# Four query projections traded for seven block products, and one weight tile prepared in its turn

## The chip, the cores and the metric

The kernel runs on one core of a Trainium2 chip. The metric is device time in microseconds (us) for one execution. Names of engines as in the profile: PE is the tensor engine, PEld its weight loads, DVE the vector engine, ACT the scalar engine, POOL the GpSimd engine, SP the engine whose queue issues most transfers.

## The reference, cut to what matters

One layer over 2048 tokens of 512 features, 32 heads of 16 and a gated feed-forward of width 1376:

```
xn = layernorm(x)
q, k, v = split(xn @ wqkv)
pq, pk  = q @ w_phi, k @ w_phi                      # per head
phi     = concat(softmax(p), softmax(-p))           # of pq and of pk
kv, z   = phi_k^T v, sum of phi_k over the tokens   # per head
s       = ((phi_q kv) / (phi_q z + 1e-6)) @ wo
gate    = xn @ W_gate; up = xn @ W_up
g       = silu((relu(gate) * up) @ W_down)
out     = x + s * g
```

The change touches how `q @ w_phi` (the products called `pq` here) is computed for half of the tokens and half of the heads. `w_phi` has been folded into the query weights before, so that `pq` is one product of `xn` with a 512 x 512 matrix, called `WQ` in the kernel.

## The kernel before, in words

**Numbers.** Each float32 operand is held as a pair of tiles, a high part and the rest (`h` and `l` in the names), and `mm3` (line 200) makes one product of three matrix multiplies: low by high, high by low, high by high. A product over 512 features takes four such steps, so 12 multiplies of 512 columns.

**Stages.** The 16 token tiles of 128 are taken in pairs. Tiles 0 to 7 in the list `order` are blocks 2 and 3 of the tokens, tiles 8 to 15 blocks 0 and 1 (a block is 512 tokens). `pair(m)` (line 1202) for m = 1 to 7 does tiles 2m and 2m+1: keys (`pk`), values (`pv`), the softmax features of the keys (`exponents`, `exp_all`, `features_k`, tile `ek`), the products of features and values (`kv_products`, `pkv`), and the transposes of coming tiles (`turn`, `pxT`). From pair 3 on, keys and values of a pair are made by seven block products where eight would be usual: the transposed input `XT` holds for a pair the four blocks A11, A12, A21, A22 (two halves of the features by two token blocks) and four sums of them S1 to S4. The sums are made when a tile is turned: DVE makes `sb`, POOL makes `xf` (`sums_more`), ACT writes the high parts (`sums_hi`) and POOL the low ones (`sums_lo`, rows `XT<-sb` and `XT<-xf`). The first block product of pair m+1 that uses a sum is S1, its second group of six multiplies (`pv<-h`).

**Queries.** `query(n)` (line 406) makes one 128-row part of `pq` for 512 tokens: 12 multiplies, one eviction by ACT into `pqs` and one or two stores to DRAM scratch (`pq<-pqs`). There are 16 of them; two stand in each pair, one in the middle (`query(n - 1)`) and one at the end (`query(n)`), and `query(N - 1)` behind the last pair. Queries 8 to 15 are of the second eight tiles; of these 10, 11, 14 and 15 are of the second half of the 512 query features. `q_load` brings the stored parts back (`pql`), and `q_pair(u)` turns two of them into attention output in many small steps on DVE, ACT and POOL.

**Feed-forward.** The width is cut into 11 tiles of 128, called f = 0 to 10. The tokens are done in two halves, blocks 0 and 1 first. For each f seven block products of six multiplies (`pa` to `pd`, in `gate_up_apart` for f = 0 and 1, in `gate_up` after that) make gate and up; DVE multiplies them (tiles `e`, `u`, later `t`, `r`), ACT and POOL split the product into `hh` and `hl`, and `down` multiplies them with W_down (`py`). Down products of f = 0 and 1 run inside f = 2, and so on. In the first half each f's weights are prepared by `f_prep` (line 542): sums and low parts on POOL (`tab`, `wa`, `wb`, `wc`, `wd`, `fdl`, ten instructions), high parts on ACT, and nine stores `ws` to DRAM, from which the second half loads them (`f_reload`).

**What sets the order.** Each engine runs its instructions in the order in which the code issues them. `Clock` (line 68) counts an estimated time while the code is written out; side work is a generator that says what its next step waits for, and `pace.pump()` issues what is due by that estimate. `preps` (`all_preps`, line 1137) is such a generator: weights of f = 0 from at = 14 on, f = 1 from 15 on, and f at N + f - 1 for the others, where `at` is the current tile number and N = 16. The tiles listed in `AHEAD` (line 36) are prepared earlier and apart: here f = 2 from at = 10 on, into a buffer of its own; it is stored and then loaded back when the first half comes to it. `queries` (`all_queries`, line 1362) holds `state()` (the last `kv_products` and the copy `kvt`), `normalizers()` (the sums `z`, `pkv<-zacc` and `pkv<-zodd`) and the `q_pair` steps.

Of the kernel before, what the change touches and what calls it, by code (L numbers as in the profile page):

```python
# [8 lines left out]
F32R = mybir.dt.float32r  # L9
# [4 lines left out]
P = 128  # L14
# [7 lines left out]
BT = 512  # L22
# [10 lines left out]
UNITS = [*(((0, j), (1, j)) for j in range(2)), ((2, 0), (2, 1)),  # L33
         *(((q, j), (q + 1, j)) for q in (6, 4) for j in range(2)), ((3, 0), (3, 1))]
LAST = [2 * q + j for q in QUERIES[1] for j in range(2)][-3:]
AHEAD, AT = (2,), (10,)
FIRST, SWAP = 3, 3
PLAN = {(0, "turned"): "gc51", (1, "split b"): "gc50", (1, "sums"): "gc01", (1, "scaled"): "gc11", (1, "mid"): "gc21", (1, "split a"): "gc00 sh01 gl01", (1, "turned"): "gc10", (2, "split b"): "sh20 sh11", (2, "sums"): "sh00 gc20", (2, "scaled"): "sh21 gl00", (2, "split a"): "gl20", (2, "turned"): "sh10 gc30 gl11", (2, "end"): "gl21 gl10", (3, "start"): "gc31 gc40 gc41", (3, "split b"): "sh30", (3, "sums"): "sh31 gl30 gl31"}

START = (14, 15)  # L40
WO_WITH = (4, 5, 6, 7)
DOWNS = {2: 1, 4: 1, 6: 1, 7: 1}

# [117 lines left out]
def layer_kernel(ctx: ExitStack, tc: tile.TileContext, x, wkT, wqT, wv, wo, wf, cst, out):  # L161
# [15 lines left out]
    def u2(shape, name, dt=F32):  # L177
        return sb.tile(list(shape), dt, tag="u2", bufs=B2, name=name)
# [222 lines left out]
    def project(n, w, name):  # L401
        p = ps(name=name)
        mm3(p, xt_cols(n), rows(w), range(KD))
        return p

    def query(n):


        h, d = divmod(n, 4)
        c = slice(h % 2 * 2 * P, (h % 2 + 1) * 2 * P)  # L410

        qs = [2 * b + h % 2 for b in PAIRS[h // 2][::-1]]
        p = ps((P, 2, 2 * P), name="pq")

        def w_of(d):
            return lambda k: [t[:, d * P:(d + 1) * P] for t in WQ[k]]
        if n < 2:
            i = 1 - n
            for d in range(2):
                mm3(p[:, d, :], w_of(d), lambda k: [XT[:, 2 * i + k // 2, s, k % 2, c] for s in range(2)], range(KD),  # L420
                    d == 0)
            to = [((qs[i], 0), slice(None), slice(None))]
        else:
            mm3(p, w_of(d), lambda k: [XT[:, k // 2:k // 2 + 3:2, s, k % 2, c] for s in range(2)], range(KD))
            to = [((q, d // 2), d % 2, i) for i, q in enumerate(qs)]
        t = u2((P, 2, 2 * P), "pqs")
        nc.scalar.activation(t, p, AF.Copy)
        for q, col, part in to:
            if q not in PQ:
                PQ[q] = dram((P, 2, 2 * P), f"pq{q[0]}{q[1]}")  # L430
            pace.when(t, lambda q=q, col=col, part=part: nc.sync.dma_start(PQ[q][:, col, :], t[:, part, :]))

    def exponents(pk):

# [107 lines left out]
    def f_prep(f, keep=True):  # L542
# [55 lines left out]
        DONE.add(f)  # L598
        yield None,

    def f_reload(f, part):
        if part == 0:
            FT[f] = [w_pair("wa"), w_pair("wb"), None, None]
            for i, t in enumerate([*FT[f][0], *FT[f][1]]):
                nc.sync.dma_start(f32(flat3(t)), wspill[f][i])
            return
        FT[f][2:] = w_pair("wc"), u2((P, 2, 2, P), "wd", F32R)
        WD[f] = u2((P, D), "fdh", F32R), u2((P, D), "fdl", F32R)
        for i, t in enumerate([*FT[f][2], FT[f][3], *WD[f]]):
            nc.sync.dma_start(f32(flat3(t)), wspill[f][4 + i])  # L610
# [153 lines left out]
    def q_load(u):  # L764
        for j, part in enumerate(UNITS[u]):
            PQS[2 * u + j] = u2((P, 2, 2 * P), "pql")
            nc.sync.dma_start(PQS[2 * u + j], PQ[part])

    def q_pair(u):
# [365 lines left out]
            STEPS[0](what)  # L1135

    def all_preps():
        for f in AHEAD:
            while at[0] < AT[AHEAD.index(f)]:
                yield 3,  # L1140
            f_load(f)
            yield 30,
            yield from f_prep(f, False)
        while at[0] < START[0] - 1:
            yield 3,
        f_load(0)
        yield 30,
        for f in range(NF):
            if f not in AHEAD:
                while at[0] < (START[f] if f < 2 else N + f - 1):  # L1150
# [51 lines left out]
    def pair(m):  # L1202

        n, c = 2 * m, cols(2 * m)
        at[0] = n

        def block(p, s, w, first):
            mm3(p, lambda k: (XT[:, s, 0, k, c], XT[:, s, 1, k, c]), rows(w), range(2), first)
            pace.pump()
        if m <= NP // 2:  # L1210
            pace.later(4, lambda: spill_x(n - 1))
        seven = m >= FIRST
        py = ps(name="pk")
        if seven:
            block(py, A11, WK[:2], True)
            px = ps(name="pk")
            nc.scalar.activation(px, py, AF.Copy)
        else:
            mm3(py, xt_cols(n), rows(WK), range(KD))
        if m > 1:  # L1220
            features_k(n - 1, *EB.pop(), engine=MULT[m > SWAP][1])
        t_steps(m, "start")
        pz = ps(name="pv")
        if seven:
            block(pz, S1, T[0], True)
            block(px, S2, T[1], False)
            va = u2((P, D), "va")
            nc.scalar.activation(va, px, AF.Copy)
        else:
            mm3(pz, xt_cols(n + 1), rows(WV), range(KD))  # L1230
        if m == 1:
            norm_apply(n + 4)
        else:
            features_split(n - 1)
        t_steps(m, "split b")
        news = [k for k in (n + 5, n + 6) if k < N]
        if news:
            norm_stats(*news, bn=m > 2)
        if seven:
            block(py, A12, WK[2:], False)  # L1240
        ea = exponents(py)
        if seven:
            block(px, S3, T[2], False)
            vb = u2((P, D), "vb")
            nc.scalar.activation(vb, px, AF.Copy)
            VH[n + 1] = u2((P, D), "v")
            add(nc.vector, by_head(VH[n + 1], True), by_head(pz), by_head(vb))
        else:
            vb = pz
        t_steps(m, "sums")  # L1250
        if news:
            norm_scale(*news)
        t_steps(m, "scaled")
        pace.pump()
        at[0] = n + 1
        if n + 3 < N:
            t = turn(n + 3)
        exp_all(ea)
        if not seven:
            features_v(n + 1, vb)  # L1260
        if n + 3 < N:
            turned(*t)
            sums_more(n + 3)
            sums_hi(n + 3, 0)
            if n + 7 < N:
                load_x(n + 7)
        t_steps(m, "mid")
        query(n - 1)
        features_k(n, ea, py, engine=MULT[m > SWAP][0])
        if n + 3 < N:  # L1270
            sums_hi(n + 3, 1)
            sums_lo(n + 3)
        for k in news:
            norm_apply(k)
        pace.pump()
        features_split(n)
        t_steps(m, "split a")
        kv_products(n - 2)
        kv_products(n - 1)
        pace.pump()  # L1280
        if seven:
            block(px, A22, T[3], False)
        else:
            px = project(n + 1, WK, "pk")
        eb = exponents(px)
        if seven:
            block(pz, S4, WV[2:], False)
            VH[n] = u2((P, D), "v")
            add(nc.vector, by_head(VH[n], True), by_head(pz), by_head(va))
        else:  # L1290
            va = project(n, WV, "pv")
        if n + 4 < N:
            t = turn(n + 4)
            if n + 8 < N:
                load_x(n + 8)
        exp_all(eb)
        t_steps(m, "turned")
        if n + 4 < N:
            turned(*t)
        if not seven:  # L1300
            features_v(n, va)
        EB.append((eb, px))
        query(n)
        t_steps(m, "end")
        pace.pump()
# [13 lines left out]
    nc.vector.memset(kvt, 0.0)  # L1319
    q_load(0)  # L1320
    query(N - 1)
    kv_products(N - 2)
    pace.pump()

    def state():
        nonlocal kvacc
        kv_products(N - 1)

        kvacc = u2((P, 256), "kvacc")
        nc.scalar.activation(kvacc, PKV[0][:, :4].rearrange("p j x -> p (j x)"), AF.Copy)  # L1330
# [65 lines left out]
    WO = None  # L1396
    for half in range(2):
        b0, b1 = 2 * half, 2 * half + 1
        for f in range(NF):
            if half == 0:  # L1400
                at[0] = N + f
                pace.finish(preps, lambda: f in DONE)
                if f == 0:
                    queries = pace.add(all_queries(0), 20)
# [122 lines left out]
```

## Time and profile before

| | us |
|---|---|
| median of 3 runs | 548.9 (548.45 to 549.0) |
| the profiled execution | 548.96 |
| its span on the core | 547.2 |
| PE busy in the span | 541.5 |
| POOL, DVE, ACT busy | 358.8, 371.3, 259.1 |

The span is the time from the first to the last instruction of the profiled execution; 1.76 us lie around it. Starts of instructions are given in us from the start of the span. A matrix multiply's busy time runs over its neighbours' (they overlap in the engine), so the work of PE is read from the distance between starts. In this execution pair 4 starts at 86.23 us, pair 5 starts at 103.42 us, pair 6 at 120.59, pair 7 at 137.28; f = 0 starts at 156.89, f = 1 at 167.35, f = 2 at 176.88.

### The profile page before, as it was taken

To read this page: it belongs to the slowest core of one execution; us is meant where nothing else is said; L and a number is where in the kernel's file an instruction comes from. 1 tells how busy PE (TensorE), PEld (TensorE's weight loads), DVE (VectorE), ACT (ScalarE), POOL (GpSimd) and SP (SyncE) were. 2 spreads that over 40 slices of the span, in tenths; PEclk is the share of its full clock that TensorE was granted. 3 is DMA by queue.
4 is the path that set the end of the run, shared out by engine and by line. 5 is a ranking of instruction groups with operands and counts; after the bars stand their busy time and mean duration, and the time that the engine had idled before them with its cause. 6 is when DMAs were issued, how large, how long until landed. Compare 5 with 4: busy or idle time off the path is not lost.

```text
span 547.2 us, 9180 instructions
## 1 busy us (share of the span) xinstructions
PE 541.5 (99%) x3192; PEld 442.0 (81%) x3192; DVE 371.3 (68%) x580; ACT 259.1 (47%) x462; POOL 358.8 (66%) x318
## 2 busy tenths in 40 slices
PE   9999999999999999999999999999999999999997
PEld 8798888888878787878878888887777887878886
DVE  5987778686559387799833432899999494924323
ACT  3688766565442657355443241244354545342510
POOL 1569994779992899999977235172365765842491
PEclk9999999999999999999999999999999999999999
DMA  8329889638999848789697998692664744657073
GB/s 281 147 104 332 180 214 266 163 94 234 265 292 394 314 148 300 260 301 330 210 323 257 406 416 320 245 356 83 217 217 134 245 140 157 230 173 288 0 232 115
DMA packets 77662, 128.34 MB, mean 235 GB/s; under 512 B 6832, under 2 KB 29232, under 8 KB 76720
## 3 DMA queue, kind: packets, MB, share of 16 engines
q1 hardware_dynamic: 75456, 120.35, 62.3%
q0 software_dynamic: 2016, 7.34, 7.5%
q8 instruction: 25, 0.41, 0.3%
q14 instruction: 21, 0.17, 0.1%
q10 hardware_dynamic: 144, 0.07, 0.0%
HBM read 70.84 MB, written 52.69 MB: 226 GB/s over the span
## 4 chain that ended last, share of the span: by engine, by line
PE 79%; DVE 8%; DMA 4%; issue 4%; POOL 3%; ACT 1%; SPq 1%; POOLq 0%; ACTq 0%; DVEq 0%
PE py L60 19%; PE pk L60 9%; PE pso L60 8%; PE pd L60 8%; PE pq L60 8%; PE pa L60 7%; PE pb L60 7%; PE pv L60 5%; PE pc L60 4%; DMA ws<-fdl 2%; DVE eq L60 1%; PE pkv L60 1%; PE pnum L60 1%; POOL ez L60 1%; PE pxT L60 1%
## 5 line engine op out<-in xcount | busy, mean ns | idle before, releaser
L60 PE MATMUL py<-fdh,hl 128*128 128x512 f32 x176 | 69.0, 392 | 0.0
L60 PE MATMUL py<-fdl,hh 128*128 128x512 f32 x176 | 68.5, 389 | 0.0
L60 PE MATMUL py<-fdh,hh 128*128 128x512 f32 x176 | 68.5, 389 | 0.0
L60 PE MATMUL pa<-XT,wa 128*128 128x512 f32 x264 | 67.3, 390 | 0.0
L60 PEld LDWEIGHTS pa<-XT,wa 128*128 128x128 f32 x264 | 49.4, 188 | 10.7 <-issue 0.4
L60 DVE TENSOR_TENSOR y<-py,y 128x512 f32<-128x512 f32 x40 | 27.5, 689 | 35.5 <-PE py L60 35.4
L60 POOL TENSOR_TENSOR hl<-t,hh 128x512 fp32r<-128x512 f32 x16 | 20.7, 1296 | 40.7 <-ACT hh L60 40.1
L60 POOL TENSOR_TENSOR y<-y,ys 128x512 f32<-128x512 f32 x24 | 30.9, 1292 | 17.8 <-ACT ys L60 17.3
L60 PE MATMUL pq<-XT,wqh 128*128 128x512 f32 (+1 forms) x144 | 40.5, 367 | 0.0
L60 PEld LDWEIGHTS py<-fdh,hl 128*128 128x128 f32 x176 | 33.0, 188 | 8.4 <-issue 1.2
L60 PEld LDWEIGHTS py<-fdh,hh 128*128 128x128 f32 x176 | 33.0, 188 | 6.9
L60 PEld LDWEIGHTS py<-fdl,hh 128*128 128x128 f32 x176 | 33.0, 188 | 6.7
L60 POOL TENSOR_TENSOR ez<-eq,zB 128x1024 f32<-128x1024 f32 x16 | 38.4, 2407 | 0.1
L60 ACT ACTIVATE hh<-t 128x512 fp32r<-128x512 f32 x16 | 10.1, 633 | 57.0 <-DVE t L60 54.7
L60 DVE TENSOR_REDUCE mx<-pk 128x32 f32<-128x512 f32 x32 | 20.6, 684 | 21.2 <-PE pk L60 21.1
L60 PE MATMUL pd<-XT,wd 128*128 128x512 f32 x132 | 34.2, 393 | 0.4 <-DVE t L60 0.3
L60 PE MATMUL pd<-XT,wc 128*128 128x512 f32 x132 | 33.9, 391 | 0.0
L60 PE MATMUL pb<-XT,wb 128*128 128x512 f32 x132 | 33.6, 390 | 0.0
L60 PE MATMUL pc<-XT,wb 128*128 128x512 f32 x132 | 33.6, 390 | 0.0
L60 POOL TENSOR_TENSOR ol<-of,oh 128x512 fp32r<-128x512 f32 (+1 forms) x13 | 19.8, 1549 | 20.3 <-ACT oh L60 20.3
L60 POOL TENSOR_TENSOR hl<-e,hh 128x512 fp32r<-128x512 f32 x6 | 7.8, 1292 | 35.1 <-ACT hh L60 35.1
L60 PE MATMUL pk<-wkh,XT 128*128 128x512 f32 x88 | 30.2, 395 | 0.0
(189 smaller groups left out, 1445.0 us busy)
## 6 DMA issues: line engine op xcount, KB each, us to landing
xts<-XT SPq DMA_DIRECT2D x4, 1792.0 KB, 8.1
zacc<-ek POOLq DMA_DIRECT2D x14, 512.0 KB, 5.9
XT<-xts SPq DMA_DIRECT2D x7, 1024.0 KB, 6.7
wa<-ws SPq DMA_DIRECT2D x24, 256.0 KB, 5.0
wb<-ws SPq DMA_DIRECT2D x24, 256.0 KB, 4.1
wc<-ws SPq DMA_DIRECT2D x24, 256.0 KB, 2.9
rawg<-wf SPq DMA_DIRECT2D x22, 256.0 KB, 2.9
ws<-wc SPq DMA_DIRECT2D x22, 256.0 KB, 5.1
```

Source lines behind the costliest of these rows:

```text
L60: return self.tc.keep_in_program_order(op(*a, **k))
```

## The change

Queries 10, 11, 14 and 15 are left out of the pairs. Their results are made behind the last pair by `q_tile`: seven block products of six multiplies on A11, S2, S3, S1, A12, A22 and S4, which by then hold blocks 0 and 1 in full. Five of them are evicted by DVE, which adds them up, and two by ACT. The weights are the blocks of `WQ` and two sums of them with their high and low parts (`TQ`), which `q_sums` makes once from at = 7 on, with ten instructions on POOL and two on ACT. `AHEAD` becomes empty, so the weights of f = 2 are prepared in turn, while f = 1 runs, and stay in place for the first half. In pairs 5 to 7 `features_k` stands behind `sums_hi` and `sums_lo` (`SUMS = 5`). `kv_products(N - 2)` moves into `state()`, and `queries` is started ahead of `q_tile` with a delay of 30 where it was 20. (`TURN = 9` and `KV_END = ()` switch nothing: m is at most 7.)

```diff
-AHEAD, AT = (2,), (10,)
+AHEAD, AT = (), ()
+Q_TILES, Q_AT = ((), (1,)), 7
+SUMS = 5
...
     def query(n):
         h, d = divmod(n, 4)
+        if d // 2 in Q_TILES[h // 2]:
+            return
...
+    def q_sums(q):
+        t = u8((P, 4, 2, 2, P), "rq")
+        r, ta, tb = [t[:, k] for k in range(2)], t[:, 2], t[:, 3]
+        for k in range(KD):
+            h, l = (f32(x[:, 256 * q:256 * q + 256].rearrange("p (d x) -> p d x", d=2)) for x in WQ[k])
+            yield "gpsimd", WQ[k][1]
+            add(nc.gpsimd, r[k // 2][:, k % 2], h, l)
+        b11, b12, b21, b22 = (t[:, :, d, :] for t in r for d in range(2))
+        o = u8((P, 2, 2, 2, 2, P), "tq", F32R)
...
+        for i, x in enumerate((ta, tb)):
+            yield "scalar", x
+            nc.scalar.activation(o[:, i, 0], x, AF.Copy)
+            yield from sums_of(o[:, i, 1], x, f32(o[:, i, 0]), ALU.subtract, o)
+        TQ[q] = o
...
+    def q_tile(half, q):
...
+        pa = ps(name="pa")
+        mm3(pa, wq_part(q, 0), a_of(A11), range(2))
+        t1 = u2((P, BT), "t1")
+        nc.scalar.activation(t1, pa, AF.Copy)
+        yield
+        pb = ps(name="pb")
+        mm3(pb, w_of(0, 0), a_of(S2), range(2))
+        m = u2((P, BT), "u2")
+        add(nc.vector, m, pb, t1)
...
+        mm3(pc, w_of(1, 1), a_of(A22), range(2), first=False)
+        t2 = u2((P, BT), "t2")
+        add(nc.vector, t2, pc, m)
+        put(b1, 0, t2)
...
         query(n - 1)
-        features_k(n, ea, py, engine=MULT[m > SWAP][0])
+        if m < SUMS:
+            features_k(n, ea, py, engine=MULT[m > SWAP][0])
         if n + 3 < N:
             sums_hi(n + 3, 1)
             sums_lo(n + 3)
+        if m >= SUMS:
+            features_k(n, ea, py, engine=MULT[m > SWAP][0])
...
     query(N - 1)
-    kv_products(N - 2)
...
     def state():
         nonlocal kvacc
+        kv_products(N - 2)
         kv_products(N - 1)
...
+        if half == 0:
+            queries = pace.add(all_queries(0), 30)
+            at[0] = N
+            for q in Q_TILES[1]:
+                for _ in q_tile(1, q):
+                    pace.pump()
```

On PE, behind the last value product of pair 7 (`pv<-wvh`), there stood before the two queries 14 and 15, of which the first fence shows the last row, and the feed-forward of f = 0 with the last two sets of `pkv` in it:

```order
L60 MATMUL pq<-XT,wqh 128x512 x2
L60 MATMUL pkv<-ek,v 32x64 x16
L60 MATMUL pa<-XT,wa 128x512 x6
L60 MATMUL pb<-XT,wb 128x512 x6
L60 MATMUL pc<-XT,wb 128x512 x6
L60 MATMUL pd<-XT,wc 128x512 x3
L60 MATMUL pkv<-ek,v 32x64 x16
L60 MATMUL pd<-XT,wc 128x512 x3
```

Now the seven blocks stand there, with both sets of `pkv` inside (`tq` are the summed weights, `wqh` and `wql` the plain ones; one `kv_products` is 16 instructions here, which the trace records as 32):

```order
L64 MATMUL pb<-XT,tq 128x512 x6
L64 MATMUL pc<-XT,tq 128x512 x6
L64 MATMUL pd<-XT,tq 128x512 x6
L64 MATMUL pa<-XT,wql 128x512
L64 MATMUL pa<-XT,wqh 128x512 x2
L64 MATMUL pkv<-ek,v 32x64 x32
L64 MATMUL pc<-XT,tq 128x512 x6
L64 MATMUL pd<-XT,wql 128x512
```

What moved: 24 multiplies of `pq` are gone here and 42 of seven blocks have come, and `pkv` runs once in 32 instructions where it ran twice in 16.

On POOL, in pair 5, the sums of tile 13 (`xf`, `XT`), the scaling of the key features `ek` and the first two instructions of the preparation of f = 2 (`rawg<-rawg`) stood before like this:

```order
L60 TENSOR_TENSOR xf<-xf,sb 128x256 x2
L60 TENSOR_TENSOR rawg<-rawg 128x256 x2
L60 TENSOR_TENSOR ek<-ek,rc 128x1024
L60 TENSOR_TENSOR XT<-sb,XT 128x2x2x128
L60 TENSOR_TENSOR XT<-xf,XT 128x2x2x128
```

Now they stand like this:

```order
L64 TENSOR_TENSOR xf<-xf,sb 128x256 x2
L64 TENSOR_TENSOR XT<-sb,XT 128x2x2x128
L64 TENSOR_TENSOR XT<-xf,XT 128x2x2x128
L64 TENSOR_TENSOR ek<-ek,rc 128x1024
L64 DMA zacc<-ek 128x1024
```

What moved: the low parts of the sums now follow `xf` at once, and the preparation of f = 2 is no longer there.

On POOL, from the last instruction of the preparation of f = 1 (`fdl`) to the split of its product, there stood before only the splits of f = 0 (`hl<-e`, `hl<-u` with the first numbers), of f = 1 (second numbers) and then the preparation of f = 3:

```order
L60 TENSOR_TENSOR fdl<-rawd,fdh 128x512
L60 TENSOR_TENSOR hl<-e_2080,hh 128x512
L60 TENSOR_TENSOR hl<-u_2062,hh 128x512
L60 TENSOR_TENSOR hl<-e_2213,hh 128x512
L60 TENSOR_TENSOR tab<-rawg 128x256 x2
```

Now the ten instructions that prepare f = 2 stand between the splits of f = 0 and of f = 1:

```order
L64 TENSOR_TENSOR hl<-e_2092,hh 128x512
L64 TENSOR_TENSOR tab<-rawg 128x256 x2
L64 TENSOR_TENSOR tab<-rawg,tab 128x256 x2
L64 TENSOR_TENSOR hl<-u_2078,hh 128x512
L64 TENSOR_TENSOR wa<-rawg,wa 128x256 x2
L64 TENSOR_TENSOR wb<-tab,wb 128x512
L64 TENSOR_TENSOR wc<-tab,wc 128x512
L64 TENSOR_TENSOR wd<-rawg,wd 128x256
L64 TENSOR_TENSOR fdl<-rawd,fdh 128x512
L64 TENSOR_TENSOR hl<-e_2195,hh 128x512
```

What moved: the low part of f = 1's product now waits for the whole preparation of f = 2.

More of the change, by code (lines that the diff above doesn't have):

```diff
@@ L40 @@
 START = (14, 15)
+TURN = 9
+KV_END = ()
+SUMS = 5
 WO_WITH = (4, 5, 6, 7)
@@ L404, in project, with wq_part, put_q @@
         return p
+    def wq_part(q, d, c=0):
+        x = (2 * q + d) * P
+        return lambda k: [t[:, x:x + P] for t in WQ[2 * c + k]]
+    PUT_Q = {}
+    def put_q(q, col, t, part):
+        if q not in PQ:
+            PQ[q] = dram((P, 2, 2 * P), f"pq{q[0]}{q[1]}")
+        PUT_Q.setdefault(q, []).append(pace.when(t, lambda: nc.sync.dma_start(PQ[q][:, col, :], part)))
     def query(n):
         h, d = divmod(n, 4)
+        if d // 2 in Q_TILES[h // 2]:
+            return
         c = slice(h % 2 * 2 * P, (h % 2 + 1) * 2 * P)
@@ L415, in w_of @@
         def w_of(d):
-            return lambda k: [t[:, d * P:(d + 1) * P] for t in WQ[k]]
+            return wq_part(d // 2, d % 2)
         if n < 2:
@@ L428, in query @@
         for q, col, part in to:
-            if q not in PQ:
-                PQ[q] = dram((P, 2, 2 * P), f"pq{q[0]}{q[1]}")
-            pace.when(t, lambda q=q, col=col, part=part: nc.sync.dma_start(PQ[q][:, col, :], t[:, part, :]))
+            put_q(q, col, t, t[:, part, :])
     def exponents(pk):
@@ L599, in f_prep @@
         yield None,
+    def q_sums(q):
[7 more added lines that the diff above has]
+        o = u8((P, 2, 2, 2, 2, P), "tq", F32R)
+        yield "gpsimd", r[1]
+        add(nc.gpsimd, tb[:, 0], b12, b11, ALU.subtract)
+        add(nc.gpsimd, ta[:, 1], b22, b12, ALU.subtract)
+        yield "gpsimd", ta
+        add(nc.gpsimd, ta[:, 0], b22, tb[:, 0], ALU.subtract)
+        add(nc.gpsimd, tb[:, 1], b21, ta[:, 0], ALU.subtract)
+        for i, x in enumerate((ta, tb)):
[3 more added lines that the diff above has]
+        TQ[q] = o
@@ new lines, in layer_kernel, with w_of, put @@
+    TQ = {}
+    def q_tile(half, q):
+        t = TQ[q]
+        b0, b1 = PAIRS[half]
+        def w_of(i, d):
+            return lambda k: [t[:, i, x, d, k, :] for x in range(2)]
+        def put(b, col, t):
+            for h in range(2):
+                put_q((2 * b + h, q), col, t, t[:, 256 * h:256 * h + 256])
+        pa = ps(name="pa")
[7 more added lines that the diff above has]
+        add(nc.vector, m, pb, t1)
+        yield
+        pc = ps(name="pc")
+        mm3(pc, w_of(0, 1), a_of(S3), range(2))
+        e7 = u2((P, BT), "e7")
+        add(nc.vector, e7, pc, m)
+        yield
+        pd = ps(name="pd")
+        mm3(pd, w_of(1, 0), a_of(S1), range(2))
+        add(nc.vector, e7, pd, e7)
+        put(b1, 1, e7)
+        yield
+        mm3(pa, wq_part(q, 0, 1), a_of(A12), range(2), first=False)
+        nc.scalar.activation(t1, pa, AF.Copy)
+        put(b0, 0, t1)
+        yield
+        mm3(pc, w_of(1, 1), a_of(A22), range(2), first=False)
+        t2 = u2((P, BT), "t2")
+        add(nc.vector, t2, pc, m)
+        put(b1, 0, t2)
+        yield
+        mm3(pd, wq_part(q, 1, 1), a_of(S4), range(2), first=False)
+        add(nc.vector, m, pd, m)
+        put(b0, 1, m)
+        TQ[q] = None
+        if q == Q_TILES[1][-1]:
+            WQ.clear()
+        yield
@@ L766, in q_load @@
             PQS[2 * u + j] = u2((P, 2, 2 * P), "pql")
+            for g in PUT_Q.pop(part):
+                pace.finish(g)
             nc.sync.dma_start(PQS[2 * u + j], PQ[part])
@@ L1137, in all_preps @@
     def all_preps():
+        for q in Q_TILES[1]:
+            while at[0] < Q_AT:
+                yield 3,
+            yield from q_sums(q)
         for f in AHEAD:
@@ L1241, in pair @@
         ea = exponents(py)
+        if m > TURN and n + 3 < N:
+            t = turn(n + 3)
         if seven:
@@ L1255, in pair @@
         at[0] = n + 1
-        if n + 3 < N:
+        if m <= TURN and n + 3 < N:
             t = turn(n + 3)
@@ L1277, in pair @@
         t_steps(m, "split a")
-        kv_products(n - 2)
-        kv_products(n - 1)
+        if m not in KV_END:
+            kv_products(n - 2)
+            kv_products(n - 1)
         pace.pump()
@@ L1302, in pair @@
         EB.append((eb, px))
+        if m in KV_END:
+            kv_products(n - 2)
+            kv_products(n - 1)
         query(n)
@@ L1398, in layer_kernel @@
         b0, b1 = 2 * half, 2 * half + 1
+        if half == 0:
+            queries = pace.add(all_queries(0), 30)
+            at[0] = N
+            for q in Q_TILES[1]:
+                for _ in q_tile(1, q):
+                    pace.pump()
         for f in range(NF):
@@ L1402, in layer_kernel @@
                 pace.finish(preps, lambda: f in DONE)
-                if f == 0:
-                    queries = pace.add(all_queries(0), 20)
             if half == 1 and f == 0:
```

## The prediction

> **What bounds the kernel now.** I read the page's first part, then who PE waited for, then the busy times by stage.
>
> ```profile
> span 547.2 us, 9180 instructions
> PE 541.5 (99%) x3192; PEld 442.0 (81%) x3192; DVE 371.3 (68%) x580; ACT 259.1 (47%) x462; POOL 358.8 (66%) x318
> ...
> PE pidle L60 <- DVE mhalf L60: 1.1, 1, 1.1
> PE pv L60 <- POOL wvl L60: 0.3, 1, 0.3
> PE pd L60 <- DVE t L60: 0.3, 1, 0.3
> ...
> 103.42:120.59 17.17, 17.17 (x139) 14.03 (x138) 11.64 (x21) 10.45 (x19) 10.41 (x11) 1.00 0.57 125
> 120.59:137.28 16.69, 16.69 (x135) 13.64 (x134) 10.82 (x18) 8.74 (x14) 15.55 (x16) 1.00 0.79 216
> ```
>
> PE waits 1.7 us in the whole span, 1.1 of them at the very start. The last two rows are pairs 5 and 6: the stretch, its length, busy us (and instructions) of PE, PEld, DVE, ACT and POOL, the granted clock, DMA's busy share and GB/s. PE is never idle there and the clock is 1.00, while DVE and ACT have 5 to 8 us to spare in each. So what is taken from PE's row of instructions is gained, as long as the others keep up with a PE that comes earlier.
>
> **What PE sheds.** Starts of multiplies, by the timeline of PE:
>
> ```profile
> 127.75 0.48 PE L60 MATMUL pq<-XT,wql 128*128 128x512 f32 x1
> 130.68 1.10 PE L60 MATMUL pkv<-ek,v 128*32 128x64 f32 x64
> 131.71 1.65 PE L60 MATMUL pk<-th,XT 128*128 128x512 f32 x6
> 133.20 0.39 PE L60 MATMUL pv<-wvh,XT 128*128 128x512 f32 x1
> ...
> 156.31 0.65 PE L60 MATMUL pkv<-ek,v 128*32 128x64 f32 x32
> 156.89 1.65 PE L60 MATMUL pa<-XT,wa 128*128 128x512 f32 x6
> 158.38 1.52 PE L60 MATMUL pb<-XT,wb 128*128 128x512 f32 x6
> 159.74 1.52 PE L60 MATMUL pc<-XT,wb 128*128 128x512 f32 x6
> 161.87 0.65 PE L60 MATMUL pkv<-ek,v 128*32 128x64 f32 x32
> 162.46 0.96 PE L60 MATMUL pd<-XT,wc 128*128 128x512 f32 x3
> ```
>
> Six multiplies of 512 columns take 1.36 us from start to start (158.38 to 159.74), 0.227 each. Four queries go: 48 x 0.227 = 10.88 us. Seven blocks come: 42 x 0.227 = 9.52 us. The difference is 6 multiplies, -1.36 us. They are the same kind of multiply on the same `XT`, so I take the same spacing for them.
>
> The two sets of `pkv` behind the pairs become one. A set of 32 alone costs 0.58 us (156.31 to 156.89), 0.13 for the block behind it (156.89 to 158.38 is 1.49 instead of 1.36) and a gap ahead of 0.09 (159.74 and nine multiplies are 161.78, the second set starts at 161.87): 0.80 for each of the two. A joint set of 64 costs 1.03 (130.68 to 131.71), 0.13 behind it (131.71 to 133.20 is 1.49) and 0.12 ahead (127.75 and twelve multiplies are 130.47; 0.09 of the rest belong to the first of them, busy for 0.48 instead of 0.39): 1.28. So -0.32 us. The sum on PE is -1.68 us.
>
> **Pairs 5 to 7: what is late next.** A pair that is one query (2.72 us) shorter reaches the first sum product of the next pair earlier, and that needs POOL's `XT<-xf`. The rows of POOL and the PE row that waits for it, in pair 5 to 6 and in pair 6 to 7:
>
> ```profile
> 113.71 1.43 POOL L60 TENSOR_TENSOR xf<-xf,sb 128x256 f32<-128x256 f32 x2 [0.85 <-DVE sb L60]
> 115.11 1.43 POOL L60 TENSOR_TENSOR rawg<-rawg 128x256 f32<-128x256 f32 x2
> 116.51 1.93 POOL L60 TENSOR_TENSOR ek<-ek,rc 128x1024 f32<-128x1024 f32 x1
> 119.68 1.29 POOL L60 TENSOR_TENSOR XT<-xf,XT 128x512 fp32r<-128x512 f32 x1
> 121.95 0.39 PE L60 MATMUL pv<-h,XT 128*128 128x512 f32 x1
> ...
> 132.42 0.75 POOL L60 TENSOR_TENSOR wd<-rawg,wd 128x256 fp32r<-128x256 f32 x1
> 133.11 1.95 POOL L60 TENSOR_TENSOR ek<-ek,rc 128x1024 f32<-128x1024 f32 x1
> 136.25 1.31 POOL L60 TENSOR_TENSOR XT<-xf,XT 128x512 fp32r<-128x512 f32 x1
> 138.64 0.39 PE L60 MATMUL pv<-h,XT 128*128 128x512 f32 x1
> ```
>
> Pair 6: the sum ends at 119.68 + 1.29 = 120.97 and PE comes at 121.95, 0.98 of reserve. Less 2.72 that would be a wait of 1.74. But `rawg` (1.40) and `ek` (1.90) no longer stand ahead of it: 0.98 - 2.72 + 3.30 = 1.56 left. Pair 7: 138.64 - 137.56 = 1.08, less 2.72 for query 11, plus 0.69 and 1.90 for `wd` and `ek`: 0.95 left. So the new order in the pairs hides it and I cost it at nothing; with that cover gone the two waits would be 1.74 and 1.64. `ek` itself comes 2.5 us later in its pair, and its reader, `pkv`, stands a whole pair later. With f = 2's preparation ten POOL instructions, six of ACT and twelve transfers of SP's queue (three loads, nine stores) leave these stretches; none ended a wait of PE, so nothing for that. In f = 1 SP's queue now holds the nine stores where it held nine loads back of the same size.
>
> **q_sums, in pairs 3 and 4.** Ten POOL instructions: eight of 256 columns at 0.70 (half of the 1.43 above) and two of 512 at 1.29, 8.2 us; two on ACT.
>
> ```profile
> 84.08 0.88 POOL L60 DMA_DIRECT2D zacc<-ek  x1
> 88.82 1.93 POOL L60 TENSOR_TENSOR ek<-ek,rc 128x1024 f32<-128x1024 f32 x1 [3.87 <-DVE rc L60]
> ```
>
> One of them stands ahead of pair 4's sums: these end at 84.8 instead of 84.08, and PE needs them 1.36 after pair 4's start, at 87.6. The other seven small ones fill an idle 3.87 and push `ek` by about 1.5 us, to an end near 92.3, where its `pkv` stands at 96.3. ACT gets two copies of 512 columns, and in pair 5, a pair of the same make, it has 6.7 us to spare (10.45 of 17.17). I take nothing, at most 0.2.
>
> **q_tile.** DVE gets five additions of 0.69 more, ACT loses two evictions.
>
> ```profile
> 160.01 0.69 DVE L60 TENSOR_TENSOR u<-pb,t 128x512 f32<-128x512 f32 x1 [3.40 <-PE pb L60]
> ```
>
> Ahead of the same addition in f = 0 DVE was idle for 3.40 us before, so its work for the last pair ends in time. The tightest reader is the second pass of `pc`, which must not start before DVE has read the first: one block (`pa`) and the joint `pkv` lie between, 2.6 us, for three additions of 0.7. I take 0, with up to 0.6 if DVE is late. What is queued behind on DVE, f = 0's additions and the first steps of `q_pair`, comes as before.
>
> **f = 2's weights inside f = 1.** This is the one place where I see no reserve. POOL and PE:
>
> ```profile
> 159.25 1.44 POOL L60 TENSOR_TENSOR wa<-rawg,wa 128x256 fp32r<-128x256 f32 x2
> 163.83 1.30 POOL L60 TENSOR_TENSOR fdl<-rawd,fdh 128x512 fp32r<-128x512 f32 x1
> 168.36 1.29 POOL L60 TENSOR_TENSOR hl<-e,hh 128x512 fp32r<-128x512 f32 x1 [3.23 <-ACT hh L60]
> 179.34 1.29 POOL L60 TENSOR_TENSOR hl<-e,hh 128x512 fp32r<-128x512 f32 x1 [7.89 <-ACT hh L60]
> ...
> 167.35 1.52 PE L60 MATMUL pa<-XT,wa 128*128 128x512 f32 x6
> 176.88 1.55 PE L60 MATMUL pa<-XT,wa 128*128 128x512 f32 x6
> 179.36 0.96 PE L60 MATMUL pc<-XT,wb 128*128 128x512 f32 x3
> ```
>
> Before, POOL was idle for 7.89 us there. Now, from f = 1's start T: `hl<-e` of f = 0 from T + 1.0 (168.36 - 167.35) to 2.3; the two pairs of `tab` 1.43 and about 1.6, to 5.3; `hl<-u` 6.6; `wa` to `fdl` 163.83 + 1.30 - 159.25 = 5.88, to 12.5; `hl<-e` of f = 1 to 13.8. PE: f = 1 takes 9.53 (167.35 to 176.88) plus the `pkv` of the normalizers, which moves in from f = 2 and costs 1.12 (179.36 less 176.88 less 1.36): f = 2 starts at T + 10.65; after `pa`, `pc` and three `py` of f = 0, 3.40 together, it wants that `hl` at T + 14.05. Reserve 0.25. But two of the first `q_pair` steps now stand on DVE ahead of f = 0's product and can push the whole by 0.4. I take +0.15; the ends are 0 and, if the raw weights land late, 2 (the rival below).
>
> **A wait that may go.**
>
> ```profile
> 205.76 0.93 PE L60 MATMUL pd<-XT,wd 128*128 128x512 f32 x3 [0.27 <-DVE t L60]
> ```
>
> This wait came from a run of `q_pair` steps on DVE, which the new order breaks up and moves by one f. Gone it gives -0.27; but such steps can meet another multiply as well. I take -0.1.
>
> **Sum.** 548.96 (profiled execution) - 1.36 - 0.32 + 0.15 - 0.1 = 547.33. The median before is 0.06 lower, so 547.3.
>
> **Rivals.** First, small waits eat most of the gain: PE comes up to 5.44 us earlier and five places have 0.25 to 1.6 us of reserve; one of 0.5 to 1.6 us in all, by a DVE that comes late at `q_tile` (0.6), pair 7's sum (up to 1) or the split in f = 2, gives 547.9 to 548.9. For it speaks how thin the reserves are; against it, that each came out positive.
>
> Second, slower: f = 2's raw weights come too late. Their load stands in SP's queue behind `zodd`, which waits for the last accumulation into `zacc`. The row of its issue, and two rows of the transfers in the window 140 to 175 us (number, size, median us to landing):
>
> ```profile
> 156.81 0.88 POOL L60 DMA_DIRECT2D zacc<-ek  x1 [0.72 <-issue]
> ...
> zacc<-ek POOLq DMA_DIRECT2D x3, 512.0 KB, 7.6
> rawg<-wf SPq DMA_DIRECT2D x4, 256.0 KB, 4.6
> ```
>
> Pair 7 comes 5.44 us (two queries) earlier, so the accumulation is issued near 151.4, lands 7.6 later near 159, the load goes out near 160.5 (four issues behind it) and lands 4.6 later near 165. f = 1 starts near 165.7 (167.35 less 10.88 for four queries, plus 9.52 for the blocks, less 0.32 for the joined `pkv`), and POOL wants the weights 2.3 later, near 168. Each us beyond that is one us of PE. It crosses today's time by 0.2% when it lands 3 us after it is wanted, near 171, which is 6 us later than these medians make it; then 550 or more.
>
> Third, the tensor engine is not the bound, so six multiplies fewer move nothing: 549.0. Weight loads are busy 81% only, which speaks for it; the even spacing of 0.227 us without a wait in pairs 5 and 6 speaks against it. The Trainium skill, "Trainium Kernel Development and Optimization", section Performance Expectations, calls matmul busy time "a bad metric" and goes by weight-load busy time; by that the 99% would hide room and the sum would be 0 instead of -1.68. The spacing in this trace decides for me against it.
>
> **Chances.** Forecast with its gain kept within half a us, 0.55, and a little better by lost waits, 0.05; small waits 0.22; not the bound 0.03; slower by late weights 0.1, by something unseen 0.05. 0.2%, 1.1 us, is about what a measurement of this kernel can tell from no change: faster 0.60, same 0.25, slower 0.15. The likeliest case's own range is 546.9 to 547.8. The range of 8 in 10 reaches down to 546.5 (no added wait, all of the 0.27 and some noise) and up to 549.8, into the slower case.
>
> **What would show it.** PE's `pa` of f = 1 near 165.7 and of f = 2 near 176.3; no PE wait on POOL at `pv<-h` in pairs 6 and 7; PE's wait for `hl` at the first `py` of f = 1 under 0.3; POOL without idle time in f = 1 up to `hl<-e`. Wrong would be a PE wait of over half a us at any of these, or POOL idle at `tab` for `rawg`.

## The result: 0.34% faster, and only in part for the reasons in the sum

The changed kernel takes 546.76 us (546.56 to 547.05, five runs), the kernel before, timed beside it, 548.9 us. The ratio is 0.9966, interval 0.9955 to 0.9977. A second measurement gave 0.9969 (0.9955 to 0.9982); its profiled execution ran at a granted clock of 0.71 and is left out below. The forecast was 547.3, so the number is good; a large part of what stands behind it is not.

The profiled execution took 546.74 us for a span of 545.0. The head of the page and all that PE waited for:

```profile
span 545.0 us, 9140 instructions
PE 539.6 (99%) x3186; PEld 440.5 (81%) x3186; DVE 372.4 (68%) x585; ACT 258.7 (47%) x462; POOL 366.9 (67%) x328
...
PE pidle L64 <- DVE mhalf L64: 1.1, 1, 1.1
```

The span is 2.2 us shorter and PE's busy time 1.9. No wait of PE is listed any more but the first; the 0.3 for `wvl` and the 0.3 for `t` are gone. Read alone, this looks like a sum that came out. The starts of the stages tell another story. On PE's timeline, kernel before (the stages of f = 0 to 2 stand in the prediction: 156.89, 167.35, 176.88):

```profile
97.35 1.65 PE L60 MATMUL pk<-th,XT 128*128 128x512 f32 x6
193.09 1.52 PE L60 MATMUL pa<-XT,wa 128*128 128x512 f32 x6
327.92 0.39 PE L60 MATMUL pso<-woh,ol 128*128 128x512 f32 x1
```

and after, pair 4's first `pk<-th`, then the first `pa` of f = 0, 1, 2 and 3, and the first `pso`:

```profile
96.24 1.65 PE L64 MATMUL pk<-th,XT 128*128 128x512 f32 x6
...
155.52 1.52 PE L64 MATMUL pa<-XT,wa 128*128 128x512 f32 x6
...
165.34 1.53 PE L64 MATMUL pa<-XT,wa 128*128 128x512 f32 x6
...
176.14 1.52 PE L64 MATMUL pa<-XT,wa 128*128 128x512 f32 x6
...
191.33 1.52 PE L64 MATMUL pa<-XT,wa 128*128 128x512 f32 x6
...
325.63 0.39 PE L64 MATMUL pso<-woh,ol 128*128 128x512 f32 x1
```

| stretch | before | after | difference | forecast |
|---|---|---|---|---|
| start to pair 4's `pk<-th` | 97.35 | 96.24 | -1.11 | 0 |
| from there to f = 1 | 70.00 | 69.10 | -0.90 | -1.68 |
| f = 1 to f = 3 | 25.74 | 25.99 | +0.25 | +0.15 |
| f = 3 to the first `pso` | 134.83 | 134.30 | -0.53 | -0.1 |

Behind the first `pso` the two are equal to 0.1 us. Half of the gain in this pair of executions lies in the first 97 us. All of it is there at pair 3's first `pk<-th` (80.17 and 79.06), and up to that place PE has the same instructions in both kernels. The part that the change rebuilt gives 0.65 of the forecast 1.53.

**The start.** DVE's normalization of the second tile and POOL's first split of `wv`, before and after:

```profile
12.98 1.58 DVE L60 TENSOR_SCALAR xt<-xt,bm,br 128x512 f32<-128x512 f32 x1
12.99 2.72 POOL L60 TENSOR_TENSOR wvl<-wvr,wvh 128x512 fp32r<-128x512 f32 x2
```

```profile
12.59 0.55 DVE L64 TENSOR_SCALAR xt<-xt,bm,br 128x512 f32<-128x512 f32 x1
12.89 2.64 POOL L64 TENSOR_TENSOR wvl<-wvr,wvh 128x512 fp32r<-128x512 f32 x2 [0.33 <-ACT wvh L64]
```

The same DVE instruction takes 1.58 us when POOL begins within 0.01 us of it, and 0.55 when DVE is 0.3 us ahead. The row of POOL holds two `wvl`; the first takes 1.28, so it ends at 14.27 and DVE 0.29 later: DVE seems to have stood until POOL's instruction ended. PE later waits 0.29 for `wvl`, and pair 4 comes 1.11 later. Not all of that is this meeting: 0.39 is there already at PE's first `pk` (10.60 before, 10.21 after; between 9.98 and 10.62 in the other traces).

**The rebuilt part.** Pair 7 of the changed kernel, PE and ACT:

```profile
133.32 0.39 PE L64 MATMUL pv<-h,XT 128*128 128x512 f32 x1
133.84 0.50 PE L64 MATMUL pk<-h,XT 128*128 128x512 f32 x1
```

```profile
131.15 1.06 ACT L64 ACTIVATE ek<-ek 128x1024 f32<-128x1024 f32 x1 [1.90 <-DVE ek L64]
132.11 0.57 ACT L64 ACTIVATE pqs<-pq 128x512 f32<-128x512 f32 x1
132.59 0.71 ACT L64 ACTIVATE wa<-rawg 128x256 fp32r<-128x256 f32 x2
133.21 0.58 ACT L64 ACTIVATE pk<-pk 128x512 f32<-128x512 f32 x1
```

A multiply is followed by the next after 0.227 us; here it takes 0.52, and 0.11 more are lost behind it. `pk<-h` accumulates on the copy `pk<-pk` that ACT makes of the first block, and that ends at 133.21 + 0.58 = 133.79. Ahead of the copy in ACT's queue stand the two `wa<-rawg` of f = 0's preparation, 0.71 us. In the kernel before they stood behind it:

```profile
138.84 0.58 ACT L60 ACTIVATE pk<-pk 128x512 f32<-128x512 f32 x1 [0.64 <-PE pk L60]
141.56 0.60 ACT L60 ACTIVATE va<-pk 128x512 f32<-128x512 f32 x1 [2.14 <-PE pk L60]
142.05 0.72 ACT L60 ACTIVATE wa<-rawg 128x256 fp32r<-128x256 f32 x2
```

So the change, by way of the estimated time that places the side work, moved these two instructions to a place where PE waits for what stands behind them. The list of waits doesn't show it. In f = 0, PE and DVE:

```profile
162.32 1.52 PE L64 MATMUL pc<-XT,wc 128*128 128x512 f32 x6
163.88 1.63 PE L64 MATMUL pd<-XT,wd 128*128 128x512 f32 x6
```

```profile
160.48 0.69 DVE L64 TENSOR_TENSOR e<-pc,u 128x512 f32<-128x512 f32 x1
161.09 0.72 DVE L64 STREAM_TRANSPOSE pq<-pql 128x512 f32<-128x512 f32 x1
161.84 1.29 DVE L64 TENSOR_REDUCE mx<-pq 128x32 f32<-128x512 f32 x2
163.05 0.68 DVE L64 TENSOR_TENSOR e<-pd,e 128x512 f32<-128x512 f32 x1
```

`pd<-XT,wd` accumulates in `pd` once `e<-pd,e` has read it (163.05 + 0.68 = 163.73). It could have run behind `e<-pc,u`, but the transposition of `pq` and its two reductions, the first steps of `q_pair`, stand ahead with 2.0 us. The six multiplies ahead of it take 1.56 instead of 1.36, with 0.10 lost behind. With two short ones in pair 6, 0.11 and 0.07, whose cause stays open, these places give back 0.88 of the 1.68 us that PE's row sheds up to f = 1; by the table 0.78 are missing there, so 0.1 came back elsewhere.

### The profile page after: what moved, and what is told of

Its sections match the earlier page's. It is cut to its first block, busy times and chain, and to the rows that moved or that the text cites. A ratio compares the mean times of both kernels' runs of the same rounds, so it can differ in the third digit from the quotient of the medians.

```text
span 545.0 us, 9140 instructions
## 1 busy us (share of the span) xinstructions
PE 539.6 (99%) x3186; PEld 440.5 (81%) x3186; DVE 372.4 (68%) x585; ACT 258.7 (47%) x462; POOL 366.9 (67%) x328
## 4 chain that ended last, share of the span: by engine, by line
PE 90%; DVE 6%; issue 1%; DMA 1%; POOL 1%; ACT 0%; DVEq 0%; POOLq 0%; ACTq 0%
PE py L64 20%; PE pd L64 10%; PE pa L64 10%; PE pk L64 9%; PE pb L64 9%; PE pso L64 8%; PE pc L64 6%; PE pq L64 6%; PE pv L64 5%; PE pkv L64 2%; PE pfold L64 1%; PE pnum L64 1%; PE pxT L64 1%; DVE qs L64 1%; DMA wb<-ws 1%
## 5 line engine op out<-in xcount | busy, mean ns | idle before, releaser
L64 PE MATMUL pq<-XT,wqh 128*128 128x512 f32 (+1 forms) x112 | 30.6, 360 | 0.0
L64 DVE TENSOR_TENSOR pb<-pb,t 128x512 f32<-128x512 f32 x16 | 11.1, 696 | 28.4 <-ACT pd L64 28.3
```

Source lines behind the costliest of these rows:

```text
L64: return self.tc.keep_in_program_order(op(*a, **k))
```

## The experiments

All ratios are to the kernel before, timed beside each variant; with them stands the stretch from pair 4's first `pk<-th` to f = 3 in the one profiled execution, which leaves the start out (before 95.74, after 95.09).

**The kernel before once more.**

> The kernel before, unchanged, for a second trace of its first 25 us. In the first pair of traces the multiply pv<-wvh,XT starts at 20.31 us before and at 19.64 after, and the one behind it 1.11 us earlier after, although both kernels issue the same instructions there. Theory A, a meeting that this program always has: DVE's 128x512 xt<-xt,bm,br again takes about 1.58 us (0.55 in the other kernel) beside POOL's wvl<-wvr,wvh, and the span is again near 547.2. Theory B, chance of one execution: it takes near 0.55, the first pk<-th of pair 3 starts near 79.1 instead of 80.17, and the span is near 546.1.

```profile
13.00 0.55 DVE L60 TENSOR_SCALAR xt<-xt,bm,br 128x512 f32<-128x512 f32 x1
13.18 2.75 POOL L60 TENSOR_TENSOR wvl<-wvr,wvh 128x512 fp32r<-128x512 f32 x2 [0.22 <-ACT wvh L60]
```

Span 546.8. DVE came 0.18 us ahead and took 0.55; pair 3's `pk<-th` was at 79.47 instead of 80.17. So the meeting at the start is chance of one execution (theory B), and it costs 0.70 here, since PE's first `pk` stands at 10.62 as before. The span fell by 0.4 only: PE lost 0.16 again up to f = 2 and 0.12 from there to f = 3.

**The start's meeting forbidden, in the kernel before.**

```diff
     norm_vector_apply(1)
+    add(nc.gpsimd, small(1, "gd", 1), XN[1][:, 0:1], XN[1][:, 0:1])
```

> The kernel before with one more POOL instruction of 128x1, which reads xt behind DVE's normalization and stands ahead of POOL's first wvl. So POOL can't start wvl while DVE still has xt to do. If the meeting of these two costs the kernel before its 1.11 us: xt<-xt,bm,br takes 0.55, the time falls by 0.7 to 1.1 us (ratio near 0.9985) and half of what the change gained is no gain of the change. If the start differs by the arrival of the first loads alone: the time stays (1.000), xt may be shorter, and PE's start is late by the same 0.4 us or so at pk.

0.9999 (0.9984 to 1.0013). `xt` took 0.55 and pair 4's `pk<-th` came at 96.28, as in the changed kernel; the time did not follow. The profiled execution had a span of 548.5, for a reason that no earlier trace had shown:

```profile
178.07 1.65 PE L60 MATMUL pa<-XT,wa 128*128 128x512 f32 x6 [2.11 <-DMA wa<-ws]
```

PE waited 2.11 us at f = 2 for its weights loaded back. The issue of that load, in the first trace and in this one:

```profile
170.51 1.71 SPq L60 DMA_DIRECT2D wa<-ws  x2
```

```profile
171.11 1.73 SPq L60 DMA_DIRECT2D wa<-ws  x2
```

The page before has the usual time from issue to landing of such a load:

```profile
wa<-ws SPq DMA_DIRECT2D x24, 256.0 KB, 5.0
```

The two halves were issued from 170.51 to 172.22 and wanted at 176.88, so the second had about 5 us. In the kernel before once more the same load was issued at 170.49, and PE's loading of weights for f = 2 stood 0.43 us for it, until 176.33. When it landed in the first trace isn't shown; with the same time it was there some 0.3 us before PE wanted it (176.66). A listed wait of zero was no reserve there. The change drops this load.

**The same in the changed kernel**, and the changed kernel again beside it.

> The changed kernel with the small POOL instruction ahead of its first wvl, which keeps POOL's wvl from starting ahead of DVE's xt. In the traces so far xt<-xt,bm,br took 1.57 to 1.61 us in three of five executions without this instruction, and pair 3's first pk<-th then started at 79.7 to 80.2 instead of 79.1 to 79.5. Theory: xt takes 0.55 in every execution, mean time 0.3 to 0.6 us lower than the changed kernel's in the same call, highest run nearer to the lowest. Rival (POOL's wvl comes later by what it saves): no difference.

> The changed kernel again, beside its variants. Ratio to the kernel before near 0.9966, as measured first. Theory (the start of a program differs by chance from execution to execution): the first pk<-th of pair 3 may now start anywhere between 79.0 and 80.2 us. Rival (the changed program has the better start always): 79.1 again.

0.9960 (0.9946 to 0.9974) with the small instruction, 0.9969 (0.9955 to 0.9982) without: no difference that could be measured. Over all runs DVE's `xt` took 1.57 to 1.61 in three of eleven profiled executions without that instruction, and 0.55 in the rest. So the start's 1.11 us belong to this pair of executions; in the mean the meeting is a few tenths at most (0.70 in three of eleven, by my estimate 0.2).

**The old order in the pairs.**

```diff
-SUMS = 5
+SUMS = 99
```

> The changed kernel with the old order in pairs 5 to 7: features_k stands ahead of the sums' splits again. My theory (the new order covers what a pair shorter by a query would wait): f = 2's preparation is gone in any case, so only ek's 1.93 us stands ahead of XT<-xf again; reserve 1.56 - 1.93 in pair 6 and 0.95 - 1.93 in pair 7, PE waits of about 0.4 and 1.0 us at pv<-h for POOL's XT<-xf, time 1.0 to 1.5 us longer than the changed kernel (548.0 to 548.3). Rival (the order doesn't matter, DVE's and ACT's own chains set the pace): no wait at pv<-h over 0.1 and the time within 0.3 us of the changed kernel's 546.8; the wait of 0.3 at pk<-h in pair 7 would go then, since DVE's reductions come earlier.

0.9982 (0.9973 to 0.9991), some 0.9 us slower than the changed kernel, a little under the 1.0 to 1.5 expected; the stretch is 96.20, 1.11 longer.

```profile
119.93 0.50 PE L64 MATMUL pv<-h,XT 128*128 128x512 f32 x1 [0.62 <-POOL XT L64]
...
135.17 0.50 PE L64 MATMUL pv<-h,XT 128*128 128x512 f32 x1 [1.00 <-POOL XT L64]
```

The two waits that the prediction's two reserves give with `ek` alone ahead are there, 0.62 and 1.00 for 0.37 (1.93 - 1.56) and 0.98 (1.93 - 0.95). `features_k` behind the sums is what keeps POOL ahead of PE.

**Six more multiplies.**

```diff
         mm3(pa, wq_part(q, 0), a_of(A11), range(2))
+        mm3(pa, wq_part(q, 0), a_of(A11), range(2))
```

> The changed kernel with the first of the seven block products computed twice (six more multiplies, the first result is overwritten). If PE's row of multiplies is the bound, as the sum has it: 6 x 0.227 = 1.36 us more than the changed kernel, less at most 0.3 of waits that the extra time covers: 547.8 to 548.1. If PE is not the bound there: 546.8.

0.9991 (0.9981 to 1.0001), 0.0025 or 1.4 us above the changed kernel's 0.9966 (0.9955 to 0.9977); the forecast was 1.36. The trace says it more sharply. Pair 4's first `pk<-th` and f = 0:

```profile
96.91 1.65 PE L64 MATMUL pk<-th,XT 128*128 128x512 f32 x6
...
157.57 1.52 PE L64 MATMUL pa<-XT,wa 128*128 128x512 f32 x6
```

That is 60.66 us where the changed kernel has 59.28, 1.38 more. PE's row is the bound there, and a multiply has its price.

**All but the seven products.**

```diff
-Q_TILES, Q_AT = ((), (1,)), 7
+Q_TILES, Q_AT = ((), ()), 7
```

> All of the change but q_tile: the four queries are back in pairs 5 to 7, the seven products are gone, and f = 2's weights are prepared in turn. My sum without the six multiplies: -0.32 (pkv) + 0.15 (split in f = 1) - 0.1 = -0.3 us against the kernel before, ratio 0.9995. A new theory: the kernel before loads f = 2's weights back, and in one execution (the one with the small POOL instruction) PE waited 2.11 us for that load at f = 2's first pa, in two others it did not. If that wait is there by chance in a part of its executions, the variant without the load back is faster by that mean as well: 0.997 to 0.9985.

0.9965 (0.9949 to 0.9980), lower than both expectations and no slower than the whole change, with nine spans from 545.2 to 545.8. The stretch is 95.53: the seven products gain 0.44 us on it in the first trace, and lose 0.15 in the trace with the small instruction (95.68), instead of 1.36.

This variant also measures the joined `pkv`, since up to f = 1 it has as many 512-column multiplies as the kernel before:

```profile
96.36 1.65 PE L64 MATMUL pk<-th,XT 128*128 128x512 f32 x6
...
166.00 1.52 PE L64 MATMUL pa<-XT,wa 128*128 128x512 f32 x6
```

From pair 4's `pk<-th` to f = 1 it takes 69.64 us, and so does the next variant. The kernel before, its repeat, its variant with the small instruction and the one-line variant below take 70.00. So the joined set gains 0.36, for -0.32 in the sum.

**That, with f = 2 prepared ahead and loaded back.**

```diff
-AHEAD, AT = (), ()
+AHEAD, AT = (2,), (10,)
```

> As the variant without q_tile, with f = 2's weights prepared ahead in pairs 5 to 7 and loaded back again, as the kernel before does; new order in the pairs stays. If the load back is a wait by chance: 0.999 to 1.000 against the kernel before, slower than the variant that prepares in turn by 0.5 to 1 us, and its runs spread as the kernel before's do (2 us). If only my sum holds: the two variants are within 0.3 us of each other.

0.9984 (0.9972 to 0.9996). PE waits at f = 2's first `pa`:

```profile
176.47 1.66 PE L64 MATMUL pa<-XT,wa 128*128 128x512 f32 x6 [1.07 <-DMA wa<-ws]
```

The stretch is 96.80, and mean spans are 546.57 against 545.36: the load back costs 1.2 us here, more than the 0.5 to 1 expected. Its lowest span of twelve, 545.9, is above the other's highest of nine, 545.8. So it is not a rare wait: the spans suggest that every run has it, with changing length, and the one trace shows it.

**One line of the change in the kernel before.**

```diff
-AHEAD, AT = (2,), (10,)
+AHEAD, AT = (), ()
```

> The kernel before with one line of the change: f = 2's weights are prepared in turn inside f = 1 and not loaded back. My sum of the prediction costs this at +0.15 us (the split in f = 1), ratio 1.000. The theory formed since: this removes a wait for the load back that comes by chance, 1.2 us in the mean (the two variants without the seven products differ by that: mean spans of 545.4 and 546.6 us), so 0.9975 to 0.9985, and the spread of its runs falls under 1 us.

0.9987 (0.9978 to 0.9997), nearer to the second expectation, of which it misses the size. The trace lists no wait but the first, the stretch is 95.75 and from f = 3 to the first `pso` it has 134.30, as the changed kernel and every variant of it (134.83 before, 134.87 in its repeat and with the small instruction): so the 0.53 us there come without the products. They don't need the preparation in turn either, since the variant above that prepares f = 2 ahead has 134.30 as well (from 192.87 to 327.17). This one line and the rest of the change without it each move the `q_pair` steps off that place. The spans still spread over 1.6 us, from 545.4 to 547.0, where under 1 was expected: the load back was not all of the chance in this kernel, and what the rest is stays open.

**The two waits of the seven products taken away**, one each and both.

```diff
-START = (14, 15)
+START = (15, 15)
```

> The changed kernel with the preparation of f = 0's weights begun one step later, so that ACT's two copies wa<-rawg (0.71 us) no longer stand ahead of pair 7's copy pk<-pk, for which PE waits about 0.40 us there (133.32 to 133.84 and the step behind it). Theory: the stretch from pair 4's first pk<-th to f = 0 falls from 59.28 to 58.9, the time by 0.4 us. Rival (the copy is late for another reason, DVE's exponents ahead of ACT's ek): the stretch stays at 59.3.

```diff
-            queries = pace.add(all_queries(0), 30)
+            queries = pace.add(all_queries(0), 45)
```

> The changed kernel with the first steps of q_pair on DVE put off by 15 matmul times, out of f = 0. Theory: PE's wait for DVE's e<-pd at pd<-XT,wd in f = 0 (0.16 us in one execution, 0.76 in another, with the transposed pq and its two reductions ahead of it on DVE) goes; f = 0 to f = 1 takes 9.6 to 9.7 us instead of 9.82 to 10.38 and the time falls by 0.2 to 0.7. Rival: the steps meet a multiply in f = 1 or f = 2 instead, and the time stays within 0.2.

> Both of these delays together in the changed kernel. If the six multiplies saved were given back by the waits in pair 7 and f = 0: 0.6 to 1.1 us under the changed kernel, ratio to the kernel before 0.995, and lower than the variant without the seven products (0.9965). If the waits only move: 0.9965 to 0.997.

The first gave 0.9976 (0.9965 to 0.9987). Pair 7's wait went (from pair 4's to pair 7's `pk<-th` it takes 45.23 us instead of 45.66), and to f = 0 it takes 58.85, as expected. But the time did not fall: f = 2's raw weights now come late, the stretch is 96.69, and PE waits twice:

```profile
96.26 1.65 PE L64 MATMUL pk<-th,XT 128*128 128x512 f32 x6
...
164.63 1.52 PE L64 MATMUL pa<-XT,wa 128*128 128x512 f32 x6
...
169.93 1.43 POOL L64 TENSOR_TENSOR tab<-rawg 128x256 f32<-128x256 f32 x2 [3.00 <-DMA rawg<-wf]
```

```profile
PE py L64 <- POOL hl L64: 0.9, 1, 0.9
PE pc L64 <- DVE e L64: 0.9, 1, 0.9
```

Up to f = 1 (164.63) this trace has 68.37 us, where the sum gives 70.00 - 1.68 = 68.32. So the six multiplies' gain is there nearly in full at that place, 1.27 of 1.36 against the variant without the products (69.64), and is lost behind it, at the place that the prediction's second rival names. The load of these weights was issued at 164.06, at 162.11 in the changed kernel and at 161.38 with both delays; why, stays open. This variant's runs spread from 546.1 to 548.7 us, and the profiled one, 548.3, is among the long ones.

The second gave 0.9966 (0.9955 to 0.9978), stretch 95.27, so the time stayed: f = 0's wait at `pd` went, and a new one of 0.27 came in `q_tile`, since the joint `pkv` no longer stands between the two passes of `pc`. Both together gave 0.9959 (0.9945 to 0.9973), 546.19 us, the lowest median of all, and the shortest stretch, 94.68:

```profile
96.11 1.65 PE L64 MATMUL pk<-th,XT 128*128 128x512 f32 x6
...
151.40 1.65 PE L64 MATMUL pc<-XT,tq 128*128 128x512 f32 x6 [0.25 <-DVE e L64]
...
190.79 1.52 PE L64 MATMUL pa<-XT,wa 128*128 128x512 f32 x6
```

The 0.25 us in the middle row come with the moved `pkv`. Against the variant without the products, 95.53, they now gain 0.85 of their 1.36; that variant was not run with the delays. The intervals of this version and of the changed kernel overlap, so the trace shows this, not the times.

## Why the prediction was right, and where its sum was not

- **The price of a multiply held.** 42 against 48 at 0.227 us: six more cost 1.4 us where 1.36 was said, 1.38 by the trace, and the rival by which PE is not the bound fell.
- **The gain of the six multiplies did not stay.** The step that failed is `q_tile`'s sentence that what is queued on DVE in f = 0 "comes as before", and the "I cost it at nothing" for pairs 5 to 7, where I looked at POOL alone. ACT's copy in pair 7 (0.40) and DVE's first `q_pair` steps in f = 0 (0.30) took it, with 0.18 in pair 6. With `START` one step later both of these waits were gone, and the gain stood nearly in full at f = 1. The first rival, small waits eat most of the gain, described this part; its total did not come, as the next two points made up for it.
- **f = 2's weights were costed on the wrong side.** The step took +0.15 for POOL's split in f = 1, which is what came (PE lost 0.2 at the second `py`), and nothing for the load back that goes. Its wait was 0, 0.2 and 2.3 us in three executions of the old order (f = 1 to f = 2 takes 9.53, 9.69 and 11.79), and 1.2 in the mean of one pair of variants.
- **The wait at 205.76** was given -0.1 and brought -0.53. The wait listed with 0.27 is 0.43 by the starts (205.10 to 205.76 for one multiply of 0.23); the other 0.1 may lie in the place where `pnum` split those six multiplies, and no run shows it. It goes with f = 2 prepared ahead as well, so it isn't a gain of the preparation in turn alone.
- **The joined `pkv`** was given -0.32 and brought -0.36 up to f = 1 (69.64 for 70.00); 0.22 of it are left at f = 3, where the variant without the products is at 95.53 and the one-line variant at 95.75.
- **The new order in the pairs** did what its two sums say, as the old order's two waits show.
- **Late raw weights.** f = 2's came in time: POOL's `tab` follows `hl` without a pause. With `START` one step later they did not (3.00 us of waiting at `tab`). And the same mechanism one f earlier is what moved f = 0's wait. In the changed kernel ACT stood for f = 1's raw weights, in the first trace and in the one with the small instruction:

```profile
154.68 0.42 ACT L64 ACTIVATE wa<-rawg 128x256 fp32r<-128x256 f32 x1 [2.33 <-DMA rawg<-wf]
```

```profile
155.27 0.98 ACT L64 ACTIVATE wa<-rawg 128x256 fp32r<-128x256 f32 x2 [2.90 <-DMA rawg<-wf]
...
159.61 0.58 ACT L64 ACTIVATE t<-pa 128x512 f32<-128x512 f32 x1
```

  Landing 0.59 later, they hold ACT's `t<-pa` to 159.61 (159.02 in the first), DVE behind it, and PE:

```profile
164.47 1.62 PE L64 MATMUL pd<-XT,wd 128*128 128x512 f32 x6 [0.59 <-DVE e L64]
```

  The late weights and the `q_pair` steps make this wait together. With the first delay ACT's `t<-pa` came at 156.67, and PE did not wait although the `q_pair` steps stood there; with the second the steps were gone, and PE did not wait at `pd` although `t<-pa` came at 159.23.

- **What would show it**: f = 1 came at 165.34 and f = 2 at 176.14, for 165.7 and 176.3. They agree by accident: without the start's 1.11 they are 0.75 and 0.95 late. No wait at `pv<-h`, and POOL without idle time from `tab` up to `hl<-e` in f = 1, were right.

So the total of -1.9 us is best made up from the two variants without the products, which were timed together. With f = 2 prepared ahead the time is -0.9 us (0.9984, with 0.7 to either side), and the traces show -0.36 for the joined `pkv` and -0.53 behind f = 3, -0.89 together. With f = 2 prepared in turn it is another -1.0 (0.9965; 1.2 by the mean spans), which is the load back. The six multiplies add nothing measurable; they show in the traces once the waits beside them are cleared. One run does not fit this: by it the one-line variant should gain the 0.53 and the load back, some 1.6 us, and it gains 0.7 (0.9978 to 0.9997). Its profiled execution, 545.4, is among its shortest, and what lengthens the others stays open.

## What to carry to other kernels

A wait of zero in one trace is not a reserve: for each load on the path, compare issue, usual landing time and use, as for the load back here (about 5 us from issue to use, where 5.0 is the usual time). When PE is made to arrive earlier, go through every in-order engine for what now stands ahead of the copy or sum that PE wants, in every stage; the engine with the lowest busy share (ACT, 47%) held it here. And when a gain is as small as the spread of one execution, split the stretch at fixed instructions and undo the parts one by one; the total can be right by accident.

## What the runs showed of the hardware

The DVE instruction `xt<-xt,bm,br` of 128x512 took 0.55 us alone and 1.57 to 1.61 when POOL's 128x512 subtraction began within 0.04 us of it, and then ended some 0.3 us behind POOL's. When DVE began 0.18 and 0.30 us ahead, it kept its 0.55, and POOL's subtraction took 1.51 and 1.40 instead of 1.28. The Trainium skill, "Trainium Architecture — The Big Picture", section What this means for kernel authors, says that DVE and GpSimd share a port pair and that it is "an exclusive lock (not a bandwidth split)". The traces agree with an instruction that stands until the other is done; with a POOL instruction that must come behind DVE's, it took 0.55 in both executions.
